# A retention layer and two MLPs on one core: queries left unscaled, loads and scalings reordered, the right side moved by 32 bytes

## The chip, the cores and the metric

The kernel runs on one NeuronCore of a Trainium2 chip. The metric is the device time of one execution in microseconds. The kernel before took 1118.17 us, the median of three runs (1112.78, 1118.94, 1118.17).

## The reference

```python
for t in range(S):                                   # S = 768, per batch (4) and head (8), D = 64
    state = gamma[None, :, None, None] * state + np.einsum('bhd,bhe->bhde', k[:, :, t], v[:, :, t])
    y[:, :, t] = scale * np.einsum('bhd,bhde->bhe', q[:, :, t], state)
x = y.transpose(0, 2, 1, 3).reshape(B * S, H * D)    # 3072 x 512
h = x @ w_in;  g = np.maximum(0.01 * h, h);  x = g @ w_out        # 512 -> 2048 -> 512
h = np.maximum(x @ w2_in, 0.0);  out = h * h @ w2_out             # 512 -> 2048 -> 512
```

All arrays are float32. The products of the MLPs are made from split operands: a value is cast to a shorter format (hi) and the rest is kept beside it (lo), and three products (hi by hi, twice with a lo) stand for one.

## The kernel before

**Attention.** Time is cut into 3 chunks of 256 steps. A unit is one chunk of two heads and two batches; there are 24. Units 0 to 7 (chunk 0) run at the start, units 8 to 23 are spread over the first MLP's first two blocks. `attend` (line 197) issues, interleaved on TensorE, the scores `sc` of unit n from its queries and keys and the output `y` of unit n-1, then the state increments `inc` of unit n (from the scaled keys kn and the values v) and the state's part of `y` of unit n-1. VectorE masks the scores (line 249, `pm`) and rolls the states on (line 256). For chunk 0, `y` goes straight to a split pair: ScalarE casts it to hi (line 270) and VectorE subtracts (line 271). For later chunks ScalarE copies it to `xs` (line 275). Mask, decay and the query factor `qt` lie in the tables `tab`.

**Loads and scalings.** A unit has four parts of 128x512: queries (0), keys (1), values (2) and the keys in the other layout (3). `loads_to` (line 158) loads the parts 0, 1, 3, `value_loads_to` (line 168) part 2. `prep_to` (line 174) multiplies the queries by `qt` on VectorE (line 181) and scales part 3 on ScalarE (line 184). `follow` (line 277) issues one attention step inside the MLP, then the loads of the next keys, then of the next values, then the scaling for the next unit.

**Order.** Loads and many stores go through SP's queue (`load`, line 126), other stores through GpSimd's (`store`). In the start the order on each engine is written out (`seq`, `pin`). Later (`strict[0] = False`) a scheduler orders each engine's instructions by its own estimate of time; `aside()` (line 101) puts the instructions of a block behind the last gate (`mark`): a gate is the activation or the split that TensorE awaits next. `prep_to` is not in such a block.

**MLPs.** `emit_plain` and `emit_in` make hidden tiles (`pa`, `pd`, `pb` in PSUM) from `xh`/`xl` and the weights `wa`/`wb`; `split_g` makes the pair `gh`/`gl` (or `gg` in one tile); `emit_out` accumulates `acc` from them and the weights `wo`. The remaining four blocks (`both_block`) keep the hidden tiles as `rot` pairs and accumulate 336 products of 128x512 per block from `rot` and the weights `wu`. Weights arrive as 64-bit words (`sg`, `st`) and are cast by ScalarE and VectorE (lines 346 to 352), split (lines 377 and 378) and stored for later blocks.

**Where tiles lie.** Pools on the left begin at multiples of 64 bytes per partition (`xh`, `xl`, `wa`, `wb`, `wu`, `gg`). Pools on the right end at byte 229,344, which is 32 past a multiple of 64. The pool `o` (30,720 bytes: `g`, `gh`, `gl`, `wo`) and, after it is closed, the pool `pairs` (40,960 bytes: `ss`, `rot`) therefore begin 32 bytes past a multiple of 64, and so do all their tiles.

Of the kernel before, what the change touches and what calls it, by code (L numbers as in the profile page):

```python
# [9 lines left out]
F32 = mybir.dt.float32  # L10
# [4 lines left out]
ALU = mybir.AluOpType  # L15

B, H, S, D = 4, 8, 768, 64
P = 128
# [37 lines left out]
def retention_then_two_mlps(  # L56
# [23 lines left out]
    def swap_left():  # L80
        early.close()
        late["ps"] = ctx.enter_context(tc.tile_pool(name="ps_b", bufs=1, space=bass.MemoryType.PSUM))
        late["p"] = ctx.enter_context(tc.tile_pool(name="units", bufs=1, reuse_waits="tile"))

    def swap_right():
        right.close()
        late["r"] = ctx.enter_context(tc.tile_pool(name="pairs", bufs=1, side="right", reuse_waits="tile"))

# [30 lines left out]
    def seq(ins):  # L119

        return pin(ins) if strict[0] else ins
# [16 lines left out]
    def blocks(t):  # L138
        return t.rearrange("p (n s) -> p n s", s=CH)
# [18 lines left out]
    def loads_to(n):  # L158
        while n_load[0] < min(n, NA):
            m = n_load[0]  # L160
            if m < ND:
                load_first(m)
            else:
                for i in (0, 1, 3):
                    load_part(m, i)
            n_load[0] += 1

    def value_loads_to(n):
        n_value[0] = max(n_value[0], ND)
        while n_value[0] < min(n, NA):  # L170
            load_part(n_value[0], 2)
            n_value[0] += 1

    def prep_to(n):
        while n_prep[0] < min(n, NA):
            m = n_prep[0]
            c, p, t = units_of[m]
            q, k = raw[m][0], raw[m][3]
            if c == NC - 1:
                k = k.rearrange("p (n s) -> p n s", n=2)[:, :, 0:C - CH]  # L180
            seq(nc.vector.tensor_tensor(
                out=blocks(q), in0=blocks(q), in1=qt[p].unsqueeze(1).to_broadcast([P, T // CH, CH]), op=ALU.mult,
            ))
            seq(nc.scalar.activation(out=k, in_=k, func=AF.Copy, scale=vt[p]))
            n_prep[0] += 1

# [10 lines left out]
    def attend(score=True):  # L197

        n = n_score[0] if score else NA
        m = n_done[0] if n_done[0] < n_score[0] else -1  # L200
        n_score[0] += n < NA
        n_done[0] += m >= 0
        half = [slice(0, D), slice(D, 2 * D)]
        put = [slice(D, 2 * D), slice(0, D)]
        sets = [(i, h) for i in range(T // CH) for h in range(2)]
        runs = [[], [], [], []]
        if n < NA:
            c, p, t = units_of[n]
            q, k, v, kn = raw[n]
            at, a_tag, y_tag = (ps["s"], "sc", "inc") if c == 0 else (ps_h, "h", "h")  # L210
            sc = at.tile([P, T], F32, tag=a_tag, name="sc", bufs=2 if c == 0 else None)
            inc = at.tile([P, 4, 2, D], F32, tag=y_tag, name="inc", bufs=1 if c == 0 else None)
            for i, h in sets:
                a, o = half[h], slice(i * CH, i * CH + CH)
                runs[0].append(dict(out=sc[a, o], lhsT=k[a, o], rhs=q[a, o], start=True, stop=True))
                g, bi = divmod(i, 2)
                o = slice(bi * C + g * CH, bi * C + g * CH + CH)
                if g < 3 or c < NC - 1:
                    runs[2].append(dict(out=inc[a, g, bi], lhsT=kn[a, o], rhs=v[a, o], start=True, stop=True))
        if m >= 0:  # L220
            mc, mp, mt = units_of[m]
            mq, _, mv, _ = raw.pop(m)
            at = ps["s"] if mc == 0 else ps["a"]
            y = at.tile([P, T], F32, tag="y", name="y", bufs=2 if mc == 0 else None)
            for i, h in sets:
                a, b, o = half[h], put[h], slice(i * CH, i * CH + CH)
                runs[1].append(dict(
                    out=y[b, o], lhsT=mv[a, o], rhs=pms[m][a, o], start=i == 0, stop=True, skip_group_check=True,
                ))
                g, bi = divmod(i, 2)  # L230
                o = slice(bi * C + g * CH, bi * C + g * CH + CH)
                if g or mc:
                    runs[3].append(dict(
                        out=y[b, o], lhsT=memory(m, g)[a, bi], rhs=mq[a, o], start=False, stop=True,
                        skip_group_check=True,
                    ))
        for one, two in (runs[0:2], runs[2:4]):
            for i in range(0, len(sets), 2):
                for kw in one[i:i + 2] + two[i:i + 2]:
                    mm(**kw)  # L240
        if n < NA:
            if c == 0:
                both = x_p.tile([P, 2, T], F32, tag=("xh7", "xl7", "xh2", "xl2")[n % 4], name="pm")
                pms[n] = both[:, 0]
                sts[n] = both[:, 1].rearrange("p (k b e) -> p k b e", k=4, b=2)
            else:
                pms[n] = a_p.tile([P, T], F32, tag="pm", name="pm", bufs=1)
                sts[n] = a_p.tile([P, 3, 2, D], F32, tag="st", name="st", bufs=1)
            seq(nc.vector.tensor_tensor(  # L249
                out=blocks(pms[n]), in0=blocks(sc), in1=mk[p].unsqueeze(1).to_broadcast([P, T // CH, CH]), op=ALU.mult,  # L250
            ))
            for g in range(4 if c < NC - 1 else 3):
                if c == 0 and g == 0:
                    seq(nc.scalar.copy(memory(n, 1), inc[:, 0]))
                else:
                    seq(nc.vector.scalar_tensor_tensor(
                        out=memory(n, g + 1), in0=memory(n, g), scalar=gt[p], in1=inc[:, g],
                        op0=ALU.mult, op1=ALU.add,
                    ))
        if m >= 0:  # L260
            pms.pop(m)
            sts.pop(m)
            if mc == 0:

                kh = mp // 2
                if (mt, kh) not in xop:
                    i = ((1, 5), (6, 3))[mt][kh]
                    xop[mt, kh] = [x_p.tile([P, 2, T], F32R, tag=f"x{l}{i}", name=f"x{l}{i}") for l in "hl"]
                hi, lo = (x[:, mp % 2] for x in xop[mt, kh])
                seq(nc.scalar.copy(hi, y))  # L270
                seq(nc.vector.tensor_tensor(out=lo, in0=y, in1=hi.bitcast(F32), op=ALU.subtract))  # L271
            else:
                if mc not in xs:
                    xs[mc] = x_p.tile([P, KB, TB], F32, tag="xs", name="xs")
                nc.scalar.copy(xs[mc][:, mp, mt * T:mt * T + T], y)

    def follow():

        attend(n_score[0] < NA)
        n = n_score[0]  # L280
        loads_to(n + 2)
        value_loads_to(n + 1)
        prep_to(n + 1)

# [715 lines left out]
        load(out=tab[p], in_=tabs[p - 1])  # L1002
    load_w(0, 0)
    loads_to(NP)
    prep_to(2)
    steps = iter(())
    for n in range(ND):
        attend()
        if n < 2:
            busy(3 - n)  # L1010
        loads_to(min(n + 4, ND))
        prep_to(min(n + 3, ND))
        if n in (3, 6):
            steps = first_in(n // 6)
        for _ in range(4 if n < ND - 1 else 2):
            next(steps, None)
        if n == 2:
            load_w(1, 0)
        elif n == 5:
            load_w(0, 1)  # L1020
        if n in (5, 6):
            emit_plain(0, n - 5, 0)
# [72 lines left out]
    for b in range(NB - 1):  # L1095
        for q in range(NQ):
            more = 0 < q < NQ - 1
            if b == 0:
# [11 lines left out]
                elif q:  # L1110
                    next_piece()
                if q == 2:
                    loads_to(ND + 2)
                    value_loads_to(ND + 1)
                    prep_to(ND + 1)
                if q > 3:
                    follow()
                emit_plain(q, 1, 1)
# [85 lines left out]
        evacuate(b, 1)  # L1204
    for lay, b in ((0, NB - 1), (1, 0), (1, 1), (1, 2)):
        both_block(lay, b, here)


_OUT = ((NB, P, KB, TB), "float32")
# [2 lines left out]
def _tables():  # L1212

    gam = (1.0 - 2.0 ** (-5.0 - np.arange(H, dtype=np.float32))).astype(np.float64)
    t = np.arange(CH)
    qt = gam[:, None] ** t / np.sqrt(D)
    vt = gam[:, None] ** (CH - t)
    s, c = np.arange(CH)[:, None], np.arange(CH)[None, :]
    mask = gam[:, None, None] ** -s * (c >= s)
    tabs = np.empty((NP, P, 2 * CH), np.float32)  # L1220
    scales = np.empty((P, NP, 2), np.float32)
    tabs[:, :, 0:CH] = mask.reshape(NP, P, CH)
    tabs[:, :, CH:] = np.repeat(qt.reshape(NP, 2, 1, CH), D, axis=2).reshape(NP, P, CH)
    scales[:, :, 0] = vt.reshape(NP, P).T
    scales[:, :, 1] = np.repeat((gam ** CH).reshape(NP, 2, 1), D, axis=2).reshape(NP, P).T
    return tabs[1:], np.concatenate((tabs[0], scales.reshape(P, 2 * NP)), axis=1)
# [43 lines left out]
```

## Time and profile before

| | |
|---|---|
| runs | 1112.78, 1118.94, 1118.17 us, median 1118.17 |
| profiled execution | 1119.63 us, its span 1117.7 us |
| mean granted TensorE clock | 0.982 of 2.4 GHz |
| attention units 0 to 7 and the first products | about 0 to 52 us |
| first MLP, blocks 0 and 1, with units 8 to 23 | about 52 to 488 us |
| four blocks with `rot` | about 488 to 1117 us |

The profile is of one execution. A line of TensorE's timeline gives start, duration, the product's result and operands, how many were merged, and in brackets the idle time before it with what ended it. A product's record of 0.39 us overlaps the next one, so the pace is read from runs of many.

### The profile page before, as it was taken

The page shows a single profiled execution, that of the slowest core. Times are in us where ns is not written, and L with a number is a line of the kernel's source. Part 1 is how long each engine was busy: PE and PEld are TensorE (multiplying, and loading weights), DVE is VectorE, ACT ScalarE, POOL GpSimd, SP SyncE. Part 2 cuts the span into 40 slices and gives each one's busy share as a digit, 9 for nine tenths or more (in the row PEclk, how much of TensorE's full clock was granted, in tenths as well). Part 3 has the DMA queues.
Part 4 walks back from the last instruction along what each step waited for, and adds up shares of the span by engine and source line. Part 5 has one row for each costly group of instructions (what it writes and reads, how often), then busy time and mean ns, then how long its engine had stood idle before and what let it go on. Part 6 is the DMA issues. An engine that isn't in the chain of part 4 may idle for free.

```text
span 1117.7 us, 18330 instructions
## 1 busy us (share of the span) xinstructions
PE 1051.0 (94%) x7135; PEld 847.9 (76%) x7135; DVE 757.5 (68%) x1255; ACT 593.9 (53%) x1001; POOL 92.0 (8%) x154
## 2 busy tenths in 40 slices
PE   6898989878989979999999999999999999999998
PEld 5686767667766758888778877888888888888886
DVE  4868866777565655748788848886655768455853
ACT  3556655544455445547656546755455555455542
POOL 0011111101000001012101022200100000000000
PEclk9999989998999999999999999999999999999999
DMA  9589977897679866779989578889155866357561
GB/s 335 159 310 349 337 256 255 281 380 272 249 264 331 320 225 242 275 272 341 373 309 342 195 279 289 341 323 350 65 170 197 329 199 271 116 194 253 174 242 56
DMA packets 81013, 294.01 MB, mean 263 GB/s; under 512 B 8352, under 2 KB 8864, under 8 KB 73376
## 3 DMA queue, kind: packets, MB, share of 16 engines
q1 hardware_dynamic: 61104, 212.56, 53.5%
q0 software_dynamic: 19680, 80.23, 18.6%
q8 instruction: 56, 0.92, 0.3%
q14 instruction: 29, 0.24, 0.1%
q10 hardware_dynamic: 144, 0.07, 0.0%
HBM read 206.84 MB, written 85.98 MB: 262 GB/s over the span
## 4 chain that ended last, share of the span: by engine, by line
PE 68%; DMA 16%; DVE 7%; ACT 3%; issue 2%; SPq 1%; POOL 0%; DVEq 0%; ACTq 0%; POOLq 0%
PE acc L124 38%; PE pa L124 18%; PE pd L124 7%; DMA r<-first 4%; DMA sg<-w 4%; PE pb L124 3%; DMA of<-wflt 1%; SPq L127 1%; DMA st<-w 1%; DMA wid<-ma 1%; DMA wid<-mc 1%; DMA wa<-wid 1%; DMA wflt<-sf 1%; DMA ydr<-ss 1%; PE inc L124 1%
## 5 line engine op out<-in xcount | busy, mean ns | idle before, releaser
L124 PE MATMUL acc<-rot,wu 128*128 128x512 f32 x1344 | 314.3, 395 | 0.0
L124 PEld LDWEIGHTS acc<-rot,wu 128*128 128x128 f32 x1344 | 252.3, 188 | 61.3
L124 PE MATMUL pa<-xh,wa 128*128 128x512 f32 x576 | 185.4, 402 | 16.3 <-DVE wa L378 7.4
L124 PEld LDWEIGHTS pa<-xh,wa 128*128 128x128 f32 x576 | 109.8, 192 | 45.6 <-DVE wa L378 9.7
L808 ACT CAST rot<-gu 128x512 fp32r<-128x512 f32 x160 | 99.2, 620 | 80.1 <-PE acc L124 69.3
L809 DVE TENSOR_TENSOR rot<-gu,rot 128x512 fp32r<-128x512 f32 x160 | 109.4, 688 | 47.7 <-ACT rot L808 47.0
L124 PE MATMUL pa<-xl,wa 128*128 128x512 f32 x288 | 114.2, 396 | 0.8 <-DVE xl L271 0.8
L124 PE MATMUL acc<-gh,wo 128*128 128x512 f32 x400 | 107.1, 401 | 4.6 <-ACT gh L735 4.6
L124 PE MATMUL pa<-xh,wb 128*128 128x512 f32 x320 | 101.9, 400 | 8.5 <-DVE g L683 7.9
L124 PE MATMUL pd<-xh,wa 128*128 128x512 f32 x320 | 99.6, 392 | 7.0 <-DVE g L688 5.4
L124 PEld LDWEIGHTS acc<-gh,wo 128*128 128x128 f32 x400 | 76.6, 193 | 23.6 <-ACT gh L735 6.2
L124 PEld LDWEIGHTS pa<-xh,wb 128*128 128x128 f32 x320 | 59.4, 190 | 24.0 <-DVE g L683 10.6
L124 PEld LDWEIGHTS pd<-xh,wa 128*128 128x128 f32 x320 | 60.0, 189 | 21.5 <-ACT st L347 6.1
L124 PEld LDWEIGHTS pa<-xl,wa 128*128 128x128 f32 x288 | 55.3, 192 | 13.0 <-DVE xl L271 1.3
L809 DVE TENSOR_TENSOR rot<-gt,rot 128x512 fp32r<-128x512 f32 x64 | 44.1, 691 | 30.9 <-ACT rot L808 30.5
L124 PE MATMUL pa<-xl,wb 128*128 128x512 f32 x160 | 63.1, 395 | 0.0
L124 PE MATMUL pd<-xl,wa 128*128 128x512 f32 x160 | 62.8, 393 | 0.0
L808 ACT CAST rot<-gt 128x512 fp32r<-128x512 f32 x64 | 39.6, 621 | 38.8 <-PE acc L124 36.0
L124 PE MATMUL acc<-gl,wo 128*128 128x512 f32 x200 | 57.1, 393 | 0.2 <-DVE gl L736 0.2
L660 ACT ACTIVATE gt<-gt 128x512 f32<-128x512 f32 x48 | 30.3, 632 | 48.6 <-DVE gt L836 34.2
L124 PE MATMUL pb<-xh,wb 128*128 128x512 f32 x160 | 49.6, 391 | 1.4 <-DVE pm L249 1.4
L848 DVE TENSOR_TENSOR gu<-gu,pb 128x512 f32<-128x512 f32 x32 | 22.0, 687 | 41.3 <-PE pb L124 41.1
(146 smaller groups left out, 1683.7 us busy)
## 6 DMA issues: line engine op xcount, KB each, us to landing
wu<-wou SPq DMA_DIRECT2D x112, 512.0 KB, 6.1
wa<-wid SPq DMA_DIRECT2D x28, 1024.0 KB, 7.5
wou<-of POOLq DMA_DIRECT2D x48, 512.0 KB, 6.9
wb<-wid SPq DMA_DIRECT2D x28, 768.0 KB, 6.1
wo<-wou SPq DMA_DIRECT2D x20, 1024.0 KB, 8.6
sg<-w SPq DMA_DIRECT2D x16, 1024.0 KB, 8.4
r<-first SPq DMA_DIRECT2D x64, 256.0 KB, 5.3
st<-w SPq DMA_DIRECT2D x24, 512.0 KB, 7.8
```

The lines of the kernel that those rows point to most:

```text
L124: pin(nc.tensor.matmul(**kw))
L127: pin(nc.sync.dma_start(**io))
L660: nc.scalar.activation(out=g, in_=g, func=AF.Relu)
L808: mark[0] = nc.scalar.copy(r[:, 0], s).ins
L809: mark[1] = nc.vector.tensor_tensor(out=r[:, 1], in0=s, in1=r[:, 0].bitcast(F32), op=ALU.subtract).ins
L848: nc.vector.tensor_tensor(out=u[:, 0], in0=u[:, 0], in1=pb, op=ALU.add)
```

## The change

Queries are used unscaled; `y` is multiplied by `qt` on VectorE instead, in place over the masked scores for chunk 0 and straight into `xs` later (the table's halves are swapped, since `y` has its two heads swapped). Loads go in the order 3, 1, 0, and values before the next unit's keys. The key scaling of later units is put behind the last gate, and that of unit 8 one step later; in the start one unit less is scaled ahead. Two small tiles are added, one to each right-hand pool.

```diff
+    def even(pool):
+
+        pad = pool.tile([P, 8], F32, tag="pad", name="pad", bufs=1)
+        nc.gpsimd.memset(pad, 0.0)
+
     def swap_right():
+        even(o_p)
         right.close()
...
-                for i in (0, 1, 3):
+                for i in (3, 1, 0):
                     load_part(m, i)
...
-            q, k = raw[m][0], raw[m][3]
+            k = raw[m][3]
...
-            seq(nc.vector.tensor_tensor(
-                out=blocks(q), in0=blocks(q), in1=qt[p].unsqueeze(1).to_broadcast([P, T // CH, CH]), op=ALU.mult,
-            ))
             seq(nc.scalar.activation(out=k, in_=k, func=AF.Copy, scale=vt[p]))
...
+            def scaled(to):
+                seq(nc.vector.tensor_tensor(
+                    out=blocks(to), in0=blocks(y), in1=qt[mp].unsqueeze(1).to_broadcast([P, T // CH, CH]), op=ALU.mult,
+                ))
+
...
-                seq(nc.scalar.copy(hi, y))
-                seq(nc.vector.tensor_tensor(out=lo, in0=y, in1=hi.bitcast(F32), op=ALU.subtract))
+                scaled(ys)
+                seq(nc.scalar.copy(hi, ys))
+                seq(nc.vector.tensor_tensor(out=lo, in0=ys, in1=hi.bitcast(F32), op=ALU.subtract))
...
-                nc.scalar.copy(xs[mc][:, mp, mt * T:mt * T + T], y)
+                scaled(xs[mc][:, mp, mt * T:mt * T + T])
...
         n = n_score[0]
+        value_loads_to(n + 1)
         loads_to(n + 2)
-        value_loads_to(n + 1)
-        prep_to(n + 1)
+        with aside():
+            prep_to(n + 1)
...
-    prep_to(2)
+    prep_to(1)
...
-        prep_to(min(n + 3, ND))
+        prep_to(min(n + 2, ND))
...
                 if q == 2:
+                    loads_to(ND + 1)
+                    value_loads_to(ND + 1)
                     loads_to(ND + 2)
-                    value_loads_to(ND + 1)
-                    prep_to(ND + 1)
+                if q == 3:
+                    with aside():
+                        prep_to(ND + 1)
...
     for lay, b in ((0, NB - 1), (1, 0), (1, 1), (1, 2)):
         both_block(lay, b, here)
+    even(late["r"])
...
-    tabs[:, :, CH:] = np.repeat(qt.reshape(NP, 2, 1, CH), D, axis=2).reshape(NP, P, CH)
+    tabs[:, :, CH:] = np.repeat(qt.reshape(NP, 2, 1, CH)[:, ::-1], D, axis=2).reshape(NP, P, CH)
```

## Rows read from the trace of the kernel before

**Rows 1.** The page: busy time of each engine; the chain that ended last, by engine.
```profile
PE 1051.0 (94%) x7135; PEld 847.9 (76%) x7135; DVE 757.5 (68%) x1255; ACT 593.9 (53%) x1001; POOL 92.0 (8%) x154
...
PE 68%; DMA 16%; DVE 7%; ACT 3%; issue 2%; SPq 1%; POOL 0%; DVEq 0%; ACTq 0%; POOLq 0%
```

**Rows 2.** Busy time by stretch: five engines, granted clock, DMA share, GB/s.
```profile
84.00:112.00 28.00, 23.12 (x95) 18.27 (x93) 23.02 (x34) 18.62 (x27) 4.05 (x6) 0.94 0.96 352
...
140.00:168.00 28.00, 23.53 (x210) 18.48 (x209) 19.64 (x30) 15.24 (x22) 3.44 (x5) 0.88 0.75 258
...
202.00:230.00 28.00, 22.96 (x392) 18.33 (x392) 23.27 (x42) 16.82 (x30) 3.61 (x6) 1.00 0.82 290
230.00:258.00 28.00, 20.54 (x364) 17.13 (x365) 20.11 (x41) 13.32 (x24) 1.07 (x2) 0.82 0.93 343
...
277.00:320.00 43.00, 39.36 (x382) 31.03 (x381) 24.20 (x48) 21.20 (x41) 3.29 (x7) 0.96 0.74 261
320.00:364.00 44.00, 37.91 (x372) 28.96 (x371) 25.68 (x54) 21.27 (x42) 2.31 (x4) 0.96 0.84 304
```

**Rows 3.** TensorE's timeline: products before which it sat idle, 84 to 364 us.
```profile
94.47 0.79 PE L124 MATMUL pa<-xh,wa 128*128 128x512 f32 x1 [3.91 <-DVE wa L378]
...
156.31 0.79 PE L124 MATMUL pa<-xh,wa 128*128 128x512 f32 x1 [4.00 <-ACT wa L377]
...
204.00 0.74 PE L124 MATMUL acc<-gh,wo 128*128 128x512 f32 x2 [2.49 <-ACT gh L735]
...
254.77 0.37 PE L124 MATMUL inc<-r 64*64 64x64 f32 x2 [7.12 <-DMA r<-first]
...
292.47 0.73 PE L124 MATMUL acc<-gh,wo 128*128 128x512 f32 x2 [1.06 <-ACT gh L735]
...
311.90 0.76 PE L124 MATMUL pd<-xh,wa 128*128 128x512 f32 x2 [2.09 <-DVE g L688]
...
334.80 0.70 PE L124 MATMUL pd<-xh,wa 128*128 128x512 f32 x2 [3.27 <-DVE g L688]
```

**Rows 4.** Waits: who waited for whom; us in total, times, longest.
```profile
PE inc L124 <- DMA r<-first: 10.3, 3, 7.1
```

**Rows 5.** ScalarE's timeline around two of the key scalings (line 184).
```profile
154.11 0.72 ACT L184 ACTIVATE r<-r,tab 128x512 f32<-128x512 f32 x1 [6.85 <-DMA r<-first]
154.74 0.58 ACT L714 ACTIVATE g<-pa 128x512 f32<-128x512 f32 x1
155.22 1.03 ACT L377 CAST wa<-wf 128x1024 fp32r<-128x1024 f32 x1
...
330.54 0.62 ACT L184 ACTIVATE r<-r,tab 128x384 f32<-128x384 f32 x1 [5.85 <-DMA r<-first]
```

**Rows 6.** The chain in order of time: start, length, work.
```profile
157.57 4.93 PE pa L124 x11
...
435.26 52.53 PE acc L124 x228
...
498.69 2.72 PE pa L124 x12
...
566.75 78.40 PE acc L124 x336
```

**Rows 7.** TensorE's timeline: runs of products from the gate tiles.
```profile
268.39 2.97 PE L124 MATMUL acc<-gg,wo 128*128 128x512 f32 x12
...
437.87 1.98 PE L124 MATMUL acc<-gh,wo 128*128 128x512 f32 x8
...
441.04 0.39 PE L124 MATMUL acc<-gl,wo 128*128 128x512 f32 x1
```

**Rows 8.** Groups by line: busy us, mean ns, idle us before and its enders.
```profile
L181 DVE TENSOR_TENSOR r<-r,tab 128x512 f32<-128x512 f32 x24 | 16.5, 687 | 17.9 <-DMA r<-first 13.7 <-DMA tab<-tab 4.1
...
L270 ACT CAST xh<-y 128x512 fp32r<-128x512 f32 x8 | 4.7, 588 | 0.0
```

**Rows 9.** SP's queue: four loads of one attention step.
```profile
240.89 3.00 SPq L127 DMA_DIRECT2D r<-first  x4
```

More of the change, by code (lines that the diff above doesn't have):

```diff
@@ L260, in attend @@
         if m >= 0:
-            pms.pop(m)
+            ys = pms.pop(m)
             sts.pop(m)
+            def scaled(to):
+                seq(nc.vector.tensor_tensor(
+                    out=blocks(to), in0=blocks(y), in1=qt[mp].unsqueeze(1).to_broadcast([P, T // CH, CH]), op=ALU.mult,
+                ))
             if mc == 0:
```

## The prediction, made before the change was run

> **What bounds the kernel now.** I read the shares of the chain first: TensorE holds 68% of it and DMA transfers 16%, so the time is TensorE's work plus the places where a transfer makes TensorE wait [rows 1]. Then I cut the span into stretches. To see there: between 84 and 364 us the granted clock falls to between 0.82 and 0.96 of 2.4 GHz and the DMA engines are up to 0.96 busy, while in the long stretches behind 435 us TensorE runs without a gap [rows 2, 6]. So there are two questions: who makes TensorE wait before 435 us, and how fast its products follow each other when nothing waits.
>
> For the first, I looked at the products before which TensorE sat idle, and what ended that [rows 3]. Most end with something of ScalarE or VectorE (gh, the weights wa, the sum g). ScalarE's own timeline says why: the key scaling of line 184 stands in its queue waiting for its transfer, 6.85 us at 154 us, with the gate of line 714 and the weight copy of line 377 directly behind it [rows 5]. There are five such scalings with gates behind them between 154 and 331 us (the first and the last are shown). The keys scaled there are needed only one attention step later; the scheduler merely put them early. A second kind ends with the transfer itself: the products inc of keys and values wait for r three times, 10.3 us together, the longest 7.1 [rows 4, 3].
>
> For the second, the pace. Twelve products of pa take 2.72 us, 0.227 us each; the 336 of acc from rot take 78.40 us, 0.2333 each, with the same shape and no gap [rows 6]. The code says where these operands lie: weights and xh on the left start at multiples of 64 bytes, rot on the right 32 bytes past one. The trace has two more cases. A run of n products lasts n-1 steps and one record of 0.39 us. Eight of gh with wo, both 32 bytes past, give (1.98 - 0.39) / 7 = 0.227; twelve of gg (a multiple of 64) with wo (32 past) give (2.97 - 0.39) / 11 = 0.235 [rows 7]. So a step is longer where the two operands differ in their place within 64 bytes. That is four cases with one reading, not a proof.
>
> **The change part by part.** The profiled execution took 1119.63 us; the sum is made against that. It lies 1.5 us above the median of the runs, 1118.17, and I take 1.5 off at the end.
>
> *The pads.* All four right-hand tile kinds of TensorE (gh, gl, wo, rot) move to multiples of 64, like their partners. Rot: 336 x 2.72 / 12 = 76.16 us instead of 78.40 [rows 6], 2.24 us in each of four blocks on the uninterrupted path: -9.0. Gate tiles: the stretch of 228 products took 52.53 us, at 0.2267 it is 51.68 [rows 6], 0.85 less; for all 768 products of gh, gl and gg that is 0.85 x 768 / 228 = 2.9: -2.9, a little generous since some are among waits. Bounds of both together: 0 and -12. The two clears of pad tiles go to GpSimd, 8% busy [rows 1], and nothing waits for them: 0.
>
> By the Trainium skill, page SBUF — State Buffer, section Specifications (TRN2), SBUF is read in lines of 16 bytes, and by its section SBUF: two separate sides TensorE's port waits for no one. A start at 32 past 64 is then as good as any, both terms are 0 and the sum is 11.9 us higher. The trace does not agree: 0.2333 against 0.227 us stands in it; but that the address is the cause is my inference, so the rule returns below as a rival.
>
> *Keys scaled behind the gates.* Where the gate comes first in ScalarE's queue, line 184 has a transfer that landed one attention step before. What goes: the waits at 156 us (4.00), 204 (2.49), 292 (1.06), 312 (2.09) and 335 (3.27) [rows 3], 12.9 us. Each has an L184 in front of its gate or weight copy. I take all of it: -12.9. The scaling itself, 0.6 to 0.7 us [rows 5], stays on ScalarE. What is late next at 156 us could be the weight copy's own input; it was there when the copy's turn came, since the copy runs straight behind the gate [rows 5], and how long before these rows don't tell.
>
> *Values ahead of the next keys.* SP issues four loads in 3.00 us at 241 us, the value last [rows 9]. In front it is issued up to 2.6 us earlier and shares the engines with three loads less, 3 x 128 x 512 x 4 bytes = 0.79 MB, 2.3 us at 343 GB/s [rows 2]. So 2.6 to 4.9 us earlier: the two shorter waits (10.3 - 7.1 = 3.2) vanish, of the 7.1 I take 4: -7.2. The keys and queries that now go behind are wanted a whole step later, in which other products run.
>
> *Queries unscaled.* Line 181, 24 x 0.687 us of VectorE, falls away with 17.9 us of waits in front of it [rows 8]; as many multiplications of y come in, so VectorE's sum stays. At 94 us TensorE waited 3.91 us for VectorE's wa [rows 3], which had a line 181 before it: between 0.7 us (the multiplication alone) and 3.9, I take -1.5, near the lower end, since a cast of the weights precedes it too. Sixteen copies xs leave ScalarE; VectorE empties y instead, covered by the several us until the next step needs that bank. In the first eight steps y, its copy hi and the subtraction lo now follow one another: VectorE's fixed order makes lo wait up to 0.59 us for the copy [rows 8], 8 x 0.59 + 0.69 for the last multiplication = 5.4 us at most; against that scores start without waiting for line 181, whose waits of 17.9 us lie partly there. Bounds -4 to +5.4; +2.
>
> *Clock.* Half the time at 1.2 GHz is lost at most, that is (1 - granted clock) x length: 3.4, 5.0, 1.7 and 1.8 us in the stretches at 140, 230, 277 and 320 us [rows 2]. Behind the wait at 156 us eleven products of pa took 4.93 us instead of 2.49 [rows 6], so 2.4 is real there. These falls come behind the waits that go. I take 2.4 + 2.0 + 1.7 + 1.7 = 7.8: -7.8.
>
> *What comes back.* From 202 to 258 us the DMA moves 28 x (290 + 343) = 17.7 MB; at the fastest stretch's 352 GB/s that is 50.4 us, 5.6 less than now, while my terms there ask for 2.5 + 7.2 + 2.0 = 11.7 [rows 2]. Between 0 and 6.1 us come back; +4, since some stores can slide on. In the second block weight pieces and stores become late next: between 1.06 and 3.27 us, as the waits there now [rows 3], at each of three places; +4.
>
> **Sum**: -9.0 - 2.9 - 12.9 - 7.2 - 1.5 - 7.8 + 2 + 4 + 4 = -31.3; 1119.6 - 31.3 = 1088.3, less 1.5: 1087 us.
>
> **Rivals.** *A: transfers bind.* For it: the engines are 0.96 and 0.93 busy in the stretches at 84 and 230 us [rows 2]. Waits only change their name, the pads alone pay 11.9, and some 3 us of waits go: 1118.2 - 15 = 1103 us. Against it: at 140 and 277 to 364 us there is room. Chance 0.15.
>
> *B: the address is not the cause of the pace* (the mechanism of that page): rot is simply read by another pattern of weights. Then 1087 + 12 = 1099 us. Against it: gh with wo reaches 0.227, gg with the same wo doesn't [rows 7]. Chance 0.12.
>
> *C: the change hardly does what it says*: the scheduler still puts the scaling ahead of other work that TensorE awaits, and the right side doesn't move. Near 1115 us, chance 0.05.
>
> *D: slower.* The scaling, now behind the gate, comes too late for the products inc, which need it in the second half of each step. Place: 16 steps behind 84 us; price: where ScalarE stands for a transfer in front of it, 5.85 to 6.85 us [rows 5]. If half the steps lose 5.85, +47, against all the gains of 31: 1134 us. It decides once six of the sixteen lose that much. For it: steps behind 202 us are short; against: the scaling is 0.7 us and its keys have long landed. Chance 0.04.
>
> **How the numbers follow.** My forecast 0.64, A 0.15, B 0.12, C 0.05, D 0.04. The forecast's own spread from the bounds is about 1073 to 1099 (pads -12 to 0 are B's; clock, give-back and start some 13 us either way). The range takes in A and B: 1073 to 1107. About 0.5%, 5.6 us, is what a measurement of this kernel can tell from no change. Faster by more: forecast, A, B: 0.91. Within: C: 0.05. Slower: D: 0.04.
>
> **What would show it.** Right: acc from rot at 0.227 us, 76.2 us for 336; no wait of L184 for its transfer behind 84 us; no idle TensorE ended by r, or only once; granted clock near 1 in the stretches at 140, 277 and 320 us. Wrong: 78.4 us for 336 (B); as much idle time before 435 us with other names, the DMA share above 0.9 throughout (A); inc waiting for L184 (D); VectorE's lo at the head of TensorE's waits before 52 us (the start worse than +5).

## The result, and the profile after

The changed kernel takes 1104.06 us (median of 4; 1100.81 to 1105.90) where the kernel before took 1118.56 beside it (median of 4): ratio 0.9872 [0.9844, 0.9900]. That is 14.5 us faster. The forecast was 1087; the time lies near the upper end of the range, and the gain is less than half of the one summed up. The profiled execution took 1102.75 us, span 1101.0; against the profiled one of before it is 16.9 us shorter, so 14.4 us of the -31.3 are missing.

The page after: busy time of each engine, and the chain that ended last by engine [rows 1].

```profile
PE 1044.2 (95%) x7135; PEld 849.2 (77%) x7135; DVE 756.4 (69%) x1255; ACT 585.4 (53%) x985; POOL 91.7 (8%) x156
...
PE 67%; DMA 15%; DVE 9%; ACT 5%; issue 3%; POOL 0%; SPq 0%; DVEq 0%; ACTq 0%; POOLq 0%
```

The shares of the chain hardly moved; VectorE and ScalarE hold a little more of it. The same stretches as before [rows 2]: length, busy time of PE, PEld, DVE, ACT, POOL, granted clock, DMA share, GB/s.

```profile
84.00:112.00 28.00, 27.55 (x122) 22.37 (x121) 20.69 (x29) 16.42 (x24) 3.48 (x5) 1.00 0.89 343
140.00:168.00 28.00, 28.00 (x242) 22.83 (x241) 20.70 (x31) 17.46 (x25) 4.09 (x6) 1.00 0.80 297
202.00:230.00 28.00, 25.35 (x447) 20.74 (x449) 22.28 (x42) 16.95 (x29) 2.37 (x5) 1.00 0.95 334
230.00:258.00 28.00, 26.86 (x376) 21.95 (x366) 25.86 (x47) 13.79 (x22) 1.07 (x2) 1.00 1.03 388
277.00:320.00 43.00, 42.00 (x401) 33.20 (x400) 31.33 (x64) 24.64 (x48) 2.12 (x4) 1.00 0.91 312
320.00:364.00 44.00, 35.51 (x361) 27.29 (x360) 26.00 (x60) 18.61 (x39) 1.73 (x4) 0.93 0.78 294
```

Taken alone, five of the six look as forecast: the clock is 1.00 there and TensorE is busier than before. The last is worse than before: 35.51 us busy in place of 37.91, clock 0.93 in place of 0.96. TensorE's timeline, read as in [rows 3], shows where it sits idle now:

```profile
50.94 1.97 PE L130 MATMUL y<-pm,r 64*64 64x64 f32 x32 [4.50 <-DVE pm L252]
...
116.35 0.80 PE L130 MATMUL pa<-xh,wa 128*128 128x512 f32 x1 [3.52 <-ACT wa L388]
...
333.92 1.22 PE L130 MATMUL pb<-xh,wb 128*128 128x512 f32 x2 [2.67 <-DVE pm L252]
...
360.70 0.92 PE L130 MATMUL pa<-xh,wb 128*128 128x512 f32 x2 [3.76 <-DVE g L694]
```

None of these stood in the kernel before at this length. The 4191 products of 512 columns come in the same order, and at the same places among all 7135 products, in every kernel of this study, so the best reading is to compare when the n-th product starts. In us, from one profiled execution of each; the difference from before is in brackets, and minus is a gain:

| product | before | changed | what lies between |
|---|---|---|---|
| 1000 | 49.40 | 54.37 (+5.0) | first chunk, start |
| 1500 | 145.65 | 151.21 (+5.6) | first weights |
| 1600 | 165.35 | 163.59 (-1.8) | the wait at 156 us gone |
| 1800 | 185.64 | 188.25 (+2.6) | a new wait of 3.1 us, over at 174 |
| 2600 | 242.02 | 241.18 (-0.8) | |
| 3000 | 293.54 | 283.11 (-10.4) | the wait of inc gone |
| 3400 | 345.03 | 326.20 (-18.8) | waits at 312 and 335 us gone |
| 4000 | 407.88 | 398.24 (-9.6) | second block: given back |
| 4700 | 546.99 | 536.66 (-10.3) | |
| last | 1113.38 | 1096.66 (-16.7) | pace of rot |

So three losses are to be explained: +5 at the start, +9 between products 3400 and 4000, and a pace of rot that brought 5.9 us where 9.0 were expected. The new wait before 174 us has no experiment; ScalarE's timeline shows the same form as [rows 5], with VectorE's piece of other weights in place of a transfer at the head of the queue and the gate behind it:

```profile
172.53 1.04 ACT L388 CAST wo<-of 128x1024 fp32r<-128x1024 f32 x1 [3.44 <-DVE of L363]
173.48 0.59 ACT L725 ACTIVATE g<-pa 128x512 f32<-128x512 f32 x1
```

### The profile page after: what moved, and what is told of

It is laid out like the page before. It is cut to its first block, busy times and chain, and to the rows that moved or that the text cites. A ratio compares the mean times of both kernels' runs of the same rounds, so it can differ in the third digit from the quotient of the medians.

```text
span 1101.0 us, 18339 instructions
## 1 busy us (share of the span) xinstructions
PE 1044.2 (95%) x7135; PEld 849.2 (77%) x7135; DVE 756.4 (69%) x1255; ACT 585.4 (53%) x985; POOL 91.7 (8%) x156
## 4 chain that ended last, share of the span: by engine, by line
PE 67%; DMA 15%; DVE 9%; ACT 5%; issue 3%; POOL 0%; SPq 0%; DVEq 0%; ACTq 0%; POOLq 0%
PE acc L130 36%; PE pa L130 19%; PE pd L130 7%; PE pb L130 3%; DMA st<-w 3%; DMA sg<-w 3%; DMA wflt<-sf 2%; DMA r<-first 2%; DMA wa<-wid 2%; DMA wid<-ma 1%; DMA ydr<-ss 1%; DMA wf<-wraw 1%; ACT sf L357 1%; DVE pm L252 1%; ACT wa L454 0%
## 5 line engine op out<-in xcount | busy, mean ns | idle before, releaser
L130 PE MATMUL acc<-rot,wu 128*128 128x512 f32 x1344 | 308.4, 391 | 0.0
L130 PE MATMUL acc<-gh,wo 128*128 128x512 f32 x400 | 104.8, 394 | 0.0
L130 PEld LDWEIGHTS pd<-xh,wa 128*128 128x128 f32 x320 | 59.7, 188 | 17.1 <-ACT gt L841 1.7
```

Source lines behind the costliest of these rows:

```text
L130: pin(nc.tensor.matmul(**kw))
```

## Experiments

The kernel before ran beside each kernel, and kernels are compared by their ratio to it. Its median lay between 1116.8 and 1121.4 us. The intervals in square brackets (95%) reach 0.2 to 0.5% to either side, so the times don't tell two kernels under 0.5% apart; where a trace does, the text says so. Of each kernel one execution was profiled.

### The pads: alone, undone, and wider

`pads_only` is the kernel before with the pads; `after_nopads` the changed kernel without them; `pad96` makes them wider:

```diff
-        pad = pool.tile([P, 8], F32, tag="pad", name="pad", bufs=1)
+        pad = pool.tile([P, 24], F32, tag="pad", name="pad", bufs=1)
```

> The kernel before with the two 32-byte pads alone. If the start of the tiles sets the pace, rot products fall from 233.3 to about 229 ns as in the changed kernel (4 blocks of 336, -1.5 us each, -5.9 us), gh and gl products from about 233 to 227 (about -3 us), and the time to about 1110 us; the prediction's sum had 1106.6 by the same two terms (-11.9). If another part of the change sets the pace, rot stays at 233 ns and the time at 1118.

> The changed kernel without its pads. If the pads are worth about 8 us and nothing of it is given back, 1112 us with rot at 233 ns; the waits at 150 and 247 us stay away, and the loss of about 5 us by 54 us of the span stays. If the quicker products are eaten again by late buffers in the second block (300 to 430 us), that block gives back less here and the time is nearer 1109.

> The changed kernel with pads of 96 bytes, so that the tiles of the right side stand at the same offset in 128 bytes as those of the left. If the two operands of a product have to agree to 128 bytes, rot falls from 229.2 to 227 ns (4 x 336 x 2.2 ns = -3.0 us), gg with wo from 233 to 227 (-1 us), time about 1100. If multiples of 64 are all that counts, rot stays at 229 and the time at 1104.

Measured: 1113.17 us (0.9962 [0.9939, 0.9985]), 1108.33 (0.9927 [0.9895, 0.9958]) and 1097.08 (0.9825 [0.9785, 0.9866]). The chain in order of time (start, length, work), first the changed kernel, then `pads_only`, `after_nopads`, `pad96`:

```profile
422.94 52.48 PE acc L130 x228
...
556.42 76.92 PE acc L130 x336
```

```profile
569.00 76.91 PE acc L130 x336
```

```profile
552.09 78.40 PE acc L124 x336
```

```profile
427.05 51.68 PE acc L130 x228
...
557.17 76.18 PE acc L130 x336
```

The pace follows the pads and nothing else: 78.40 us without them, whatever else is changed, 76.92 with 32 bytes, 76.18 with 96. Per product that is 233.3, 228.9 and 226.7 ns, where the right side starts 32 bytes past a multiple of 64, 64 past one of 128, and at a multiple of 128, as the left does. The forecast's 76.16 (within 0.02 us) and its 51.68 for the 228 products from gate tiles are what 96 bytes give; with 32 bytes the gate tiles gain almost nothing (52.48 against 52.53 [rows 6]). The rival that the address has no part in the pace is out. By the Trainium skill, page SBUF — State Buffer, section Specifications (TRN2), SBUF is read in lines of 16 bytes, by which all three would be alike; the trace does not agree.

That it is the difference of the two operands' places which counts, as the forecast read [rows 7], is not shown. The eight products of gh with wo shown there are the quick ones. The eight that the same trace has just ahead of them are slower, (2.02 - 0.39) / 7 = 0.233 us a step, with the same two tile kinds:

```profile
435.10 2.02 PE L124 MATMUL acc<-gh,wo 128*128 128x512 f32 x8
```

All tiles of that pool have sizes that are multiples of 2,048 bytes, so gh and wo agree in their place within 128 bytes already in the kernel before. A rule on the difference alone would give them the quick pace there. But their mean step is 230.7 ns there, 229.6 with 32 bytes of pads, and 227.1 only with 96. Whether the place of the right side counts by itself, or a pace carries over from the products just before, stays open.

### The start: what the factor on y holds up

`late_lo` puts the subtraction lo behind the next unit's masking; `late_hi` puts the copy hi there too (its edit, shortened):

```diff
                 scaled(ys)
-                seq(nc.scalar.copy(hi, ys))
-                seq(nc.vector.tensor_tensor(out=lo, in0=ys, in1=hi.bitcast(F32), op=ALU.subtract))
+                behind_mask.append((hi, lo, ys))
```

`scaled_q` takes the unscaled queries back (line 181 and the copies of y as before) and keeps all else.

> The changed kernel with the subtraction that makes lo put behind the next unit's masking, so that VectorE doesn't wait for ScalarE's copy hi. If the serial chain y, factor, copy, subtraction is what makes the start late, the wait of 0.68 us in each of 8 units goes, TensorE's 1000th product stands 3 to 5 us earlier than in the changed kernel (54.4 us), and the end 2 to 4 us earlier (1100 to 1102). If the start is late by something else (the masking behind other work of VectorE, weights that are late), the 1000th product moves by under 1 us and the time stays at 1104.

> The changed kernel with both the copy hi and the subtraction lo of a first-chunk unit put behind the next unit's masking. Theory: ScalarE stands at the copy hi until VectorE has masked, updated three states and put the factor on y (2.5 us in each step), and what lies behind it, the activation of the first products and its copy gh, is late by that; then TensorE's 1000th product moves from about 54 to 49.5 us and the time falls by 3 to 5 us, to about 1100. Rival: the weights that arrive at 109 us set the next stretch, so that the 1000th product is early but the 1300th stays at 131 us and the time at 1104.

> The changed kernel with its queries scaled again on VectorE with the keys (behind the gates from the second chunk on), y unscaled and copied out by ScalarE; loads, keys and pads stay. Theory: the start is then as in the kernel before, TensorE's 1000th product at 49 to 50 us in place of 54, and the wait of y for VectorE at 226 us is away, so that the factor on y costs 3 to 7 us net and this runs in 1097 to 1101. Rival (the prediction's terms, -1.5 for the queries and +2 for the start): within 1 us of 1104.

Measured: `late_lo` 1104.17 us (0.9895 [0.9848, 0.9942]), its 1000th product at 56.02 us; `late_hi` 1099.51 (0.9836 [0.9814, 0.9857]), 48.86; `scaled_q` 1101.35 (0.9845 [0.9805, 0.9884]), 51.88. My first theory, VectorE waiting for the copy, fell with `late_lo`: VectorE's wait went and nothing came earlier. ScalarE's timeline of the changed kernel shows who really waits (last bracket: idle before it, and what ended that):

```profile
43.99 0.62 ACT L280 CAST xh<-pm 128x512 fp32r<-128x512 f32 x1 [2.48 <-DVE pm L268]
44.52 0.72 ACT L187 ACTIVATE r<-r,tab 128x512 f32<-128x512 f32 x1
45.14 0.66 ACT L399 ACTIVATE wf<-sg 128x512 f32<-128x512 f32 x1
...
47.39 0.57 ACT L725 ACTIVATE g<-pa 128x512 f32<-128x512 f32 x1
47.87 1.19 ACT L358 ACTIVATE sg<-sg 128x512 uint32<-128x512 uint32 x2
48.96 0.60 ACT L746 CAST gh<-g 128x512 fp32r<-128x512 f32 x1
```

In `late_hi` the same gate and its copy stand at:

```profile
43.14 0.58 ACT L732 ACTIVATE g<-pa 128x512 f32<-128x512 f32 x1
...
44.77 0.60 ACT L753 CAST gh<-g 128x512 fp32r<-128x512 f32 x1
```

The copy hi needs the multiplied y, and VectorE multiplies only after masking and three updates; ScalarE stands there for 2.48 us, with a key scaling, four operations for the weights and the gate queued behind it. gh comes 4.2 us later than in `late_hi`, and so do gl, the masking of line 252 in VectorE's fixed order, and TensorE, which idles 4.50 us at 50.94. In the kernel before that copy took y straight from PSUM and never waited [rows 8]. With hi out of the way the whole loss up to product 1000 is gone. Of these 5.5 us, 3.2 are left at product 2000, and none at product 4700 (536.66 and 536.73 us in the two profiles): `late_hi` waits 4.3 us for a transfer of r up to 249 us, the changed kernel doesn't. A weight transfer of 14 us stands in both chains ahead of the products at 116 to 119 us (95.06 to 108.97 in the changed kernel, 91.80 to 105.88 in `late_hi`). That it is what eats the first part of the gain is my reading and not tested.

### Keys and values

`keys_inline` takes `with aside():` away around `prep_to`; `values_late` undoes the order of the loads (queries, keys, next keys, then values).

> The changed kernel with its key scaling back in line, not behind the gates. By the prediction's sum the five waits of the scaling for its transfer come back (12.9 us of TensorE): 1112 to 1117, with the stalls near 150 and 204 us. Rival: with values ahead and no scaling of queries the keys stand in time in most places, and only 2 to 4 us come back: 1106 to 1108.

> The changed kernel with the order of its loads undone: queries, keys and next keys of the unit after next first, values behind them. By the prediction's sum 7.2 us come back, as waits of inc for its values at 221, 230 and 250 us: about 1111. Rival: the scaling behind the gates had already moved these waits, and most profiles of the changed kernel still show one of 2 to 4 us there, so that the order is worth 3 us at most: 1104 to 1107.

Measured: `keys_inline` 1120.47 (1.0030 [1.0012, 1.0048]), `values_late` 1106.04 (0.9890 [0.9855, 0.9925]). Without its place behind the gates the scaling costs 16 us (18 by the ratios), and the changed kernel would be 0.3% slower than the one before. ScalarE's timeline of `keys_inline` is the old picture [rows 5] again:

```profile
160.27 0.72 ACT L187 ACTIVATE r<-r,tab 128x512 f32<-128x512 f32 x1 [7.71 <-DMA r<-first]
160.90 0.58 ACT L724 ACTIVATE g<-pa 128x512 f32<-128x512 f32 x1
161.38 1.03 ACT L387 CAST wa<-wf 128x1024 fp32r<-128x1024 f32 x1
```

Between 84 and 420 us line 187 waits 13 times for its transfer there, 48.9 us together; the kernel before has ten such waits, 36.9 us, the changed kernel one, 1.2 us, and `values_late` three, 3.4 us. That the waits grew beyond those of before because the keys now travel behind the values is my inference.

The order of the loads is worth less than forecast: 2 us by the ratios, which the times don't tell from nothing. In the profile of the changed kernel no wait of inc is left near 250 us, but that is not the rule: nine of the 16 other profiles with the same order have it once, with 2.1 to 5.0 us, as in `late_hi`; and in `values_late` inc waits longer, first of all for the scaling. Waits of TensorE between 215 and 262 us (total, times, longest), `late_hi` first:

```profile
PE inc L130 <- DMA r<-first: 4.3, 1, 4.3
```

```profile
PE inc L130 <- ACT r L187: 6.1, 2, 5.5
PE inc L130 <- DMA r<-first: 1.4, 1, 1.4
```

### A new wait for y

`copy_out` lets ScalarE copy y out as before, and multiplies in place afterwards:

```diff
-                scaled(xs[mc][:, mp, mt * T:mt * T + T])
+                to = xs[mc][:, mp, mt * T:mt * T + T]
+                nc.scalar.copy(to, y)
+                y = to
+                scaled(to)
```

> The changed kernel with y of the second and third chunk copied out of PSUM by ScalarE as before, and multiplied in place afterwards. Theory: the next y waits at 226 and 236 us for VectorE's multiplication, which alone empties its buffer; that wait (2.4 + 0.9 us) goes, and the time falls to 1101 or 1102. Rival: ScalarE's extra 0.6 us for each of 16 units delays gates by as much: 1104 or up to 3 us slower.

Measured: 1101.70 (0.9848 [0.9810, 0.9886]). The waits of y between 215 and 262 us in the changed kernel, then in `copy_out`:

```profile
PE y L130 <- DVE xs L268: 3.0, 2, 2.2
PE y L130 <- DVE st L259: 0.7, 2, 0.4
```

```profile
PE y L130 <- ACT xs L286: 2.4, 2, 1.9
PE y L130 <- DVE st L259: 2.3, 3, 1.4
```

By the time alone the copy may be worth 2 to 3 us, which the intervals don't tell from nothing; by the trace the wait only changed its name (3.7 us against 4.7). So the wait for y is not shown to cost anything that this copy would save.

### The second block

Three kernels were made for the 9 us given back. `late_xs` puts the factor on y behind the next gate; `late_cast` issues the side casts of even steps (the casts of weight pieces for later blocks) behind the last gate of the quarter; `light_cast` leaves out the three VectorE operations of seven such casts.

> The changed kernel with the factor on y of the second block put behind the quarter's next gate (the sum of g with a product). Theory: the 0.60 us of that multiplication stands in the chain ahead of that gate five times between 310 and 404 us and is part of what is given back there: about -3 us (1101), the stalls at 336, 357, 382 and 404 us shorter by 0.6 each. Rival: VectorE's chain is late because casts behind it wait for transfers; then the stalls stay and the time is 1104.

> The changed kernel with the side casts of the second block (those at even steps) issued behind the quarter's last gate in place of ahead of it. Theory: a cast that waits for the store of its own buffer (12.3 and 9.5 us in flight) holds ScalarE's queue, and with it the masking and the gates: stalls at 331, 336 and 357 us go, -3 to -5 us (about 1100). Rival: the bound there is VectorE's sheer work, or transfers that then start later: 1104, or up to 4 us slower.

> The changed kernel with the three VectorE operations left out of the side casts of the second block (seven pieces, 0.42 + 0.69 + 0.69 us each; the weights stored there are then wrong). TensorE's products 3000 to 4000 (283 to 398 us) took 112 to 115 us in every kernel so far, whatever was moved. Theory: VectorE's work, in the order in which it stands ahead of the gates, is what this stretch waits for; of the 12.6 us taken away 4 to 8 come off it (108 to 111 us). Rival: casts wait for the stores of their buffers, that is for transfers; the stretch stays at 113 to 115 us.

`more_dma` adds transfers, `pool_store` moves stores to another queue:

```diff
+    extra = dram.tile([P, NQ, 512], U64, name="extra")
...
+                if b and 0 < q < 6:
+                    load(out=extra[:, q], in_=w2[q, 1][:, 0:512])
```

```diff
-            load(out=wflt[q, half][:, c], in_=stage.pop(("f", n)))
+            put = load if n < 13 else store
+            put(out=wflt[q, half][:, c], in_=stage.pop(("f", n)))
...
-            put_wid(1, FIRST[n // 2], *stage.pop(("h", n)), n % 2, load)
+            put_wid(1, FIRST[n // 2], *stage.pop(("h", n)), n % 2, store)
```

> The changed kernel with one transfer more of 512 KB, from memory to memory, in each of five quarters of the second block (1.3 us each at the 400 GB/s seen there, 6.5 us in all). Theory that VectorE's work bounds the stretch: products 3000 to 4000 take 115 us as before, within 1.5. Rival that transfers bound it: they take 4 to 6 us longer, 119 to 121.

> The changed kernel with the stores of the second block's side work (seven of 256 KB, the halves of 512 and 384 KB) put on GpSimd's queue in place of SyncE's. Theory: neither VectorE's work nor the bytes, but the 9 to 13 us that such a store is in flight behind what was queued on SyncE's queue ahead of it holds the next cast at the head of ScalarE's queue; on the other queue it lands in 5 to 8 us, and products 3400 to 4000 take 66 to 68 us in place of 69 to 72: time 1099 to 1101. Rival: the same 16 engines carry both queues and the flight stays at 9 to 13 us: stretch and time as they were.

| kernel | ratio to before | products 3000 to 3400, us | 3400 to 4000, us |
|---|---|---|---|
| before | 1 | 51.49 | 62.85 |
| changed | 0.9872 [0.9844, 0.9900] | 43.09 | 72.04 |
| `pads_only` | 0.9962 [0.9939, 0.9985] | 48.50 | 65.75 |
| `late_lo` | 0.9895 [0.9848, 0.9942] | 43.08 | 69.15 |
| `late_hi` | 0.9836 [0.9814, 0.9857] | 43.11 | 66.69 |
| `keys_inline` | 1.0030 [1.0012, 1.0048] | 45.29 | 68.93 |
| `late_xs` | 0.9866 [0.9839, 0.9894] | 43.11 | 70.82 |
| `late_cast` | 0.9834 [0.9810, 0.9859] | 42.44 | 68.48 |
| `light_cast` | 0.9870 [0.9837, 0.9902] | 42.27 | 71.27 |
| `more_dma` | 0.9838 [0.9802, 0.9874] | 43.09 | 69.27 |
| `pool_store` | 0.9786 [0.9758, 0.9814] | 44.10 | 65.82 |

First, what one profile can tell: `late_lo` and `late_hi` change nothing behind the first chunk and still take 69.15 and 66.69 us in the last column, where the changed kernel takes 72.04. So the loss there is 4 to 9 us, and single entries between 66 and 72 can't be ranked. In the changed kernel TensorE idles 12.3 us of that column (6.3 before), and the clock stands at half for 13.7 us of it (3.4 before); in `late_hi` it is 10.2 and 3.4 us. Among all profiles the slow clock goes from 3.4 to 17.1 us. The extra idle time does not go away with any one part of the change: it is 10.7 us in `keys_inline`, 10.9 in `values_late`, 11.2 in `scaled_q` and 11.4 in `after_nopads`.

The two columns together make 110 to 115 us in every kernel: what is won in the first is paid in the second. `late_xs`: the multiplication has no part in it that the time or these columns show. `light_cast`: 12.6 us of VectorE's work less over the two columns change nothing that the time shows (0.9870 against 0.9872), so it is not the amount of that work. `more_dma`: 2.6 MB more don't lengthen it, so it is not the amount of bytes either. What is left to suspect is the order in which things wait. The chain of the changed kernel goes through three stores in flight, and ScalarE stands for them with its next cast:

```profile
318.87 12.32 DMA wflt<-sf
...
344.05 9.46 DMA wflt<-sf
...
364.25 12.54 DMA wid<-ma
```

```profile
331.22 0.66 ACT L357 ACTIVATE sf<-st 128x512 f32<-128x512 f32 x1 [3.56 <-DMA wflt<-sf]
...
376.82 0.30 ACT L454 CAST ma<-wf 128x128 fp32r<-128x128 f32 x1 [5.37 <-DMA wid<-ma]
```

`late_cast` takes the first kind out of the chain, and the second takes its place: stores again up to 375 us, three of them, this time of ma (9.19, 7.03 and 12.60 us). The last two as the chain has them:

```profile
345.35 7.03 DMA wid<-ma
...
362.17 12.60 DMA wid<-ma
```

But such stores are not new. The chain of the kernel before has three between 336 and 410 us as well, and that of `late_hi` four (10.47, 9.59, 11.58 and 11.57 us) in its 66.69 us. The kernel before:

```profile
336.11 10.80 DMA wflt<-sf
...
379.54 11.44 DMA wid<-mc
...
398.04 11.70 DMA wid<-ma
```

`pool_store` is the one whose ratio lies clear of the changed kernel's. But not as I had expected: the stores of ma and mc land only 2 to 3 us sooner and those of wflt later (DMA issues of 320 to 400 us, median us to landing at the end; the changed kernel, then `pool_store`), and ScalarE still waits for wflt, 5.48 us at 360 and 6.21 at 374.

```profile
wid<-ma SPq DMA_DIRECT2D x4, 512.0 KB, 11.9
wid<-mc SPq DMA_DIRECT2D x4, 384.0 KB, 11.6
...
wflt<-sf SPq DMA_DIRECT2D x3, 256.0 KB, 3.6
```

```profile
wid<-ma POOLq DMA_DIRECT2D x4, 512.0 KB, 9.0
wid<-mc POOLq DMA_DIRECT2D x4, 384.0 KB, 9.7
wflt<-sf POOLq DMA_DIRECT2D x5, 256.0 KB, 9.9
```

So it is shown that casts waiting for the stores of their buffers stand in the chain of this stretch, before the change and after it, and that it isn't the amount of VectorE's work or of bytes. That these waits are what gives the 4 to 9 us back is not shown: the cause of the loss stays open. Moving the stores helps the changed kernel by its time; why it does, by the flight or by what queues up behind a store on SyncE's queue, stays open too.

### Putting parts together

`best` is `pad96` + `late_hi` + `late_cast`; `best_copy` adds `copy_out`; `best_all` adds `pool_store` to that; `best_q` is `pad96` + `late_cast` + `scaled_q`.

> The changed kernel with pads of 96 bytes, hi and lo of the first chunk behind the next masking, and side casts behind the gates. If the three add up (-3 to -7, -4.5, -4.5 us by their own runs), 1088 to 1092. If the start's gain and the casts' gain wait for the same transfers, 1093 to 1097.

> Pads of 96 bytes, hi and lo behind the next masking, side casts behind the gates, and y copied out of PSUM by ScalarE ahead of its multiplication. If the last adds what it gave by itself (-2.4), 1092; if the stretch around it takes that up, 1094.5 as without it.

> The four parts of the fastest kernel so far (1090.0) with these stores on GpSimd's queue too. If the flight is the cause, 1086 to 1088; if not, 1090, or slower where GpSimd's queue holds its other stores up.

> Pads of 96 bytes, side casts behind the gates, queries scaled as in the kernel before; loads and keys as in the changed kernel. If the unscaled queries cost 2.7 us in the changed kernel and the other two add up, 1089 to 1093; if the start of this kernel waits at 156 us for the same weights as the other, 1094 to 1097.

Measured: `best` 1094.55 us (0.9787 [0.9750, 0.9824]), `best_copy` 1090.00 (0.9718 [0.9689, 0.9748]), `best_all` 1089.53 (0.9721 [0.9690, 0.9753]), `best_q` 1094.38 (0.9766 [0.9737, 0.9795]). All four beat both kernels. The gains don't add up in full (by the ratios 9.5 us for three that gave 5.3, 4.0 and 4.3 alone), and the stores on the other queue, worth most alone, add nothing to `best_copy` by the time, though products 3400 to 4000 take 66.77 us in place of 71.53 in the two profiles. `best_copy`, 30.7 us below the kernel before, lies where the forecast had put the changed kernel; that is a coincidence, since it took four more edits to get there.

## Why the prediction went wrong, step by step

Four terms of the sum failed: the pads (the size), the clock (counted as a gain of its own), the start (the mechanism) and what comes back in the second block (the size). The gain from the keys was right.

**The pads, -9.0 and -2.9: the cause was right, the size wrong.** Measured -5.9 for rot (4 x 1.48) and, from the mean steps of gh, gl and gg, -0.5. The step that failed is the one that set the pace to that of pa as soon as the right side stands at multiples of 64, "like their partners". I had compared places within 64 bytes, since the rows only had a difference of 32, and of the runs of gh with wo I had taken the quick ones. The left side stands at a multiple of 128, and only `pad96` puts the right side at one too; it gives the two terms within 0.2 us (8.9 and 2.7). 5.5 us of the missing 14.4.

**Start, +2, and queries, -1.5: right place, wrong mechanism.** Measured +5.0 at product 1000, near the end of my bounds (+5.4), which I had reached by another way: I let VectorE wait for the copy. In truth ScalarE waits for VectorE, and the cost is what is queued behind ScalarE's copy. That the bound held is luck. 4.5 us more are missing here at product 1000; how many of them reach the end, the times don't settle: by the ratios `late_hi` gains 4.0 us and `scaled_q` 3.0, both within what two kernels' times can tell apart, and in the profiles of the changed kernel and of `late_hi` nothing is left of it by product 4700. No run shows a gain from unscaled queries by themselves; I had summed them and the start to +0.5.

**Keys, -12.9: right,** as to the waits that go: none of the five is left. `keys_inline` puts the place at 16 to 18 us, but with the new order of the loads, in which the scaling waits longer (48.9 us) than in the kernel before (36.9).

**Values, -7.2: about half.** The wait of 7.1 us is gone in eight of the 17 profiles with the new order and one of 2 to 5 in nine; `values_late` is 2 us slower in the median, within what the times tell apart.

**Clock, -7.8: wrong.** The dips I had listed went, and others came behind the new waits. Behind 84 us the clock stands at half for 30.6 us in place of 34.0, and in the first 84 us for 17 in place of 7; the mean granted clock fell from 0.982 to 0.978. In the four runs of the changed kernel it was 0.972 to 0.980, in those of the kernel before, beside the experiments, 0.974 to 0.988. So at most (34.0 - 30.6) / 2 = 1.7 us were gained there, 6 us less than summed. The step took the clock as a gain of its own, but it is given back with the waits that appear.

**What comes back, +4 and +4.** The forecast had the place of the second right, not the size: in the profile the second block gave back 9.2 us, more than the 6.4 us of waits that went there; 6 of the 9.2 are idle time, and the clock can account for the rest. For the first, DMA moves 388 GB/s in the stretch behind 230 us, more than the 352 I had taken as the most, and little came back; what was late next was y.

These items don't add up to 14.4 us: pads 5.5, start 4.5, clock 6, values some 3 and the second block 5 make more, less 4 of the first give-back that didn't come. They overlap, since idle time at the start and in the second block brings the clock down too. Of these only the pads' share was measured by adding them alone and by taking them away alone (`pads_only` 4.7 us in the median, `after_nopads` 6 us by the ratios).

**Rivals.** The time is that of A (1103). As a whole its reasons aren't: the scaling's place pays 16 us. But its "waits only change their name" is what the second block shows. B falls with the pads alone, and C with them and with line 187, which waits for its transfer once behind 84 us (1.2 us). D does not occur: between 84 and 420 us inc waits for the scaling not once in the changed kernel.

## To carry to other kernels

Before you credit a wait that goes, ask for the next two in line on the same engine: in an in-order queue an operation that newly depends on another engine holds up everything behind it, and that was dearer here than the operation itself. Check a stretch by when the n-th product starts, not by its shares: 277 to 320 us looked perfect, and the stretch after it lost 9 us. Before you explain such a loss, look how far it moves between kernels that are alike there: here it was 5 us. When a layout is to be aligned, test more than the smallest offset that explains the rows: 64 bytes explained them here, and 128 were needed.

## What the runs showed of the hardware

TensorE's pace depends on where the tiles of its operands start. With one operand at multiples of 128 bytes, 336 products of 512 columns without a gap take 233.3 ns each with the other 32 bytes past a multiple of 64, 228.9 at 64 past a multiple of 128 and 226.7 at a multiple of 128, within 0.03 us of the whole run in every profile with the same pads. Whether the difference of the two places or the place of the one counts is open. Where both operands lie on the right side, 32 past, the pace depends on what ran just before: behind pa the steps are uneven (236, 233, 236, 224, 231, 236, 228 ns at 435.10 us of the kernel before), and those of a run straight behind it come at 226 to 227 (437.87 us). With 96 bytes of pads both are at 226 to 227. And 2.6 MB of extra transfers from memory to memory, in a stretch where the DMA engines are 0.8 busy, cost nothing that could be measured.
